# A three-stage kernel with a written instruction order: the list reads of the last expert tiles are gathered into one step ahead of those tiles' weights, and the order is written anew

## The chip, the cores and the metric

The kernel runs on one NeuronCore of a Trainium2 chip. The metric is the device time of one execution in microseconds (us). Before the change three runs gave 534.38, 535.60 and 536.59 us; the median is 535.6. The five engines of the core each work through their own instructions in order: PE (TensorE, matrix multiplication), DVE (VectorE), ACT (ScalarE), POOL (GpSimd, which here also issues the gathers and scatters through an index list) and SP (SyncE, which issues the plain DMAs). They meet only at semaphores.

## The reference

Three stages follow each other. What is computed, cut to its core:

```python
# 1. chunked state-space attention: 4 batches, 8 heads, 768 positions, head size 32, state 16
L = exp(cum[:, None] - cum[None, :]) * causal          # inside a chunk
y = (C @ B.T * L) @ x + (C @ state) * exp(cum)
state = decay * state + (B * decay_from_j).T @ x
x = y.reshape(3072, 256)
# 2. dense layer
h = x @ w_in                                           # 256 -> 2048
x = maximum(0.01 * h, h) @ w_out                       # 2048 -> 256
# 3. one of eight experts for every token
logits = x @ w_gate + modality_bias[modality_id]
e_idx, gate = argmax(logits), softmax(logits)[e_idx]
for e in range(8):
    mask = e_idx == e
    out[mask] = gate * (maximum(x[mask] @ w1[e], 0) @ w2[e])   # 256 -> 1024 -> 256
```

## The kernel before, in words

Stage 1 goes through 24 chunks of 128 positions. Stage 2 goes through six blocks of 512 tokens, each in 16 steps of 128 hidden columns: a step `h` (L655, six matmuls; both operands are split into a high and a low part, so that three products stand for one) and a step `y` (L695, six matmuls). Chunks and blocks are interleaved. After the last `y` of a block its logits are formed, every token gets its expert and its place, and POOL scatters the token numbers into a list in DRAM (`put`, L835: four scatters of 128 numbers, 4 bytes each; the list is `il`). The token rows themselves go to a DRAM buffer `yx`.

Stage 3 takes tiles of 512 tokens of one expert. Two *early* tiles (0 and 1) are taken from the lists of the first four blocks; the *final* tiles (2 to 5 here, and more behind branches that were not taken in this trace) need the lists of all six blocks. For tile `i` the steps are:

- `ix.i` (L962 to L964, SP): reads from a small table which piece of the list the tile has, then issues the DMA of 512 list entries into `gi`. It waits for all scatters of all `put` steps so far (L965 to L969).
- `w1.i`, `w2.i` (L945 to L955, SP): the expert's number from the table, then two DMAs of 512 KB each for `w1` (256x1024) and two for `w2` (1024x256), into raw tiles. Three raw tiles exist, so a load may wait until an earlier raw tile has been converted.
- `ga.i` (L977, POOL): four gathers of 128 token rows each through `gi`, into `xg`.
- `xt.i` (L1006, PE): eight transposes of `xg` into `xps`; `xe`, `xf` (L1012 on ACT, L1016 on DVE): the high and the low part of the tokens, `x2h` and `x2l`.
- `sh1`, `sh2` (L995, ACT) and `sl1`, `sl2` (L999, DVE; the second half of `sl2` on POOL): high and low part of the weights, `w1s` and `w2s`, half by half.
- `m1.i.f` (L1025, PE, six matmuls) for eight hidden groups `f` into `hp`, of which two exist; `re.i.f` (L1039, ACT) and `rl.i.f` (L1043, DVE) make `hh` and `hl` from it and so set `hp` free; `m2.i.f` (L1056, PE, twelve matmuls) adds up the output `o`.
- `oe.i.q` (L1082, ACT) scales the output, `sc.i.q` (L1086, POOL) scatters it to the result.

Nothing is scheduled when the program is built: the string `PLAN` names all steps (1,599 of them) in one line of order, and each engine gets the instructions of a step in that order. `m1.1.3 m2.1.0` in the plan means that PE gets the twelve matmuls of `m2.1.0` behind the six of `m1.1.3`. Where an instruction waits, all that stands behind it on its engine waits too.

Of the kernel before, what the change touches and what calls it, by code (L numbers as in the profile page):

```python
# [41 lines left out]
    trc.5 exp.6.0 subv.i.2.1 cb.5 gl.6 h.8 hb.o.2.1 mul.5.0 mul.5.2 lb.o.2.1 mul.5.1 hb.i.3.0 h.9 mul.5.3 or.o.2.1  # L42
    sa.8 gh.7 y.6 gg.8 lb.i.3.0 cast.o.2.1 gl.7 h.10 sa.9 subv.o.2.1 gh.8 or.i.3.0 hb.i.3.1 trmm.6 p3.5 lb.i.3.1 gl.8
    cast.i.3.0 y.7 or.i.3.1 sa.10 load.9 exp.7.1 gg.9 subg.i.3.0 y.8 cast.i.3.1 gg.10 gh.9 mask.8 trc.6 h.11 hb.o.3.0
    subv.i.3.1 gh.10 gl.9 xa.5 h.12 gl.10 exp.6.1 xb.5 cd.8 y.9 trb.6 bs.6 sa.11 lb.o.3.0 gg.11 cb.6 sa.12 or.o.3.0
    gh.11 h.13 exp.8.0 mul.6.1 mul.6.3 y.10 mul.6.0 cast.o.3.0 mul.6.2 gg.12 sa.13 subg.o.3.0 p3.6 exp.7.0 gl.11
    trmm.7 load.10 xa.6 h.14 st.6 trb.7 trc.7 gh.12 xb.6 hb.o.3.1 bs.7 gl.12 trd.7 y.11 lb.o.3.1 gg.13 trde.7 sa.14
    or.o.3.1 cb.7 exp.8.1 h.15 mul.7.3 gh.13 mul.7.1 mul.7.2 cast.o.3.1 gl.13 y.12 sa.15 mul.7.0 mask.9 gg.14 y.13
    gg.15 gh.14 bs.8 exp.9.1 gl.14 p3.7 cd.9 subv.o.3.1 gh.15 trmm.8 load.11 st.7 xa.7 y.14 trb.8 xb.7 exp.9.0 trc.8
    gl.15 h.16 bs.9 bt h.17 sa.16 gg.16 y.15 sa.17 gh.16 gg.17 h.18 evV.0 evA.0 gh.17 gl.16 trd.8 gl.17 sa.18 h.19  # L50
    trde.8 gg.18 mask.10 lg.0 sa.19 cd.10 exp.10.0 gg.19 y.16 lt.0 exp.10.1 cb.8 y.17 gh.18 mul.8.3 mul.8.1 mul.8.0
    mul.8.2 trmm.9 gh.19 gl.18 p3.8 trb.9 trc.9 gl.19 trd.9 xa.8 load.12 l2.0 y.18 st.8 trde.9 r1.0 trmm.10 xb.8 rx.0
    trd.10 r2.0 trb.10 h.20 trde.10 mask.11 trc.10 r3.0 cb.9 sa.20 bs.10 cd.11 exp.11.1 h.21 gg.20 mul.9.2 mul.9.0
    gh.20 y.19 mul.9.1 sa.21 mul.9.3 gl.20 exp.11.0 p3.9 gg.21 gh.21 rp.0 st.9 load.13 xa.9 yr.0.0 be.0 h.22 yc.0.0
    xb.9 put.0 gl.21 yr.0.1 sa.22 bs.11 h.23 yc.0.1 gg.22 ro.0 h.24 sa.23 gg.23 trmm.11 sa.24 y.20 trc.11 trb.11
    trd.11 gh.22 y.21 trde.11 gl.22 gg.24 cb.10 gh.23 mask.12 y.22 mul.10.3 mul.10.2 exp.12.0 mul.10.1 mul.10.0 h.25
    gl.23 gh.24 exp.12.1 gl.24 p3.10 sa.25 y.23 st.10 load.14 xa.10 gg.25 xb.10 h.26 gh.25 bs.12 gl.25 cb.11 sa.26
    h.27 gg.26 mask.13 mul.11.2 mul.11.0 h.28 mul.11.3 sa.27 mul.11.1 exp.13.0 gg.27 p3.11 cd.13 sa.28 exp.13.1 y.24
    load.15 xa.11 bs.13 y.25 gh.26 xb.11 gl.26 h.29 gh.27 gg.28 gl.27 y.26 sa.29 gg.29 y.27 gh.28 gl.28 h.30 gh.29
    gl.29 h.31 sa.30 gg.30 y.28 sa.31 cd.14 mask.14 gg.31 trmm.12 gh.30 h.32 trc.12 trb.12 gl.30 exp.14.1 cb.12 sa.32  # L60
    h.33 mul.12.1 exp.14.0 mul.12.0 mul.12.3 mul.12.2 y.29 sa.33 gg.32 p3.12 gh.31 gl.31 trmm.13 xa.12 load.16 y.30
    st.12 trb.13 trc.13 mask.15 xb.12 gg.33 y.31 gh.32 bs.14 exp.15.0 gl.32 trd.13 evV.1 h.34 evA.1 cd.15 gh.33 h.35
    sa.34 gl.33 trde.13 gg.34 exp.15.1 y.32 sa.35 cb.13 gg.35 gh.34 h.36 mul.13.3 mul.13.1 mul.13.2 mul.13.0 y.33
    sa.36 gl.34 gg.36 lg.1 gh.35 gl.35 p3.13 lt.1 l2.1 st.13 xa.13 load.17 yr.1.0 r1.1 h.37 yc.1.0 r2.1 rx.1 trmm.14
    sa.37 r3.1 rp.1 trb.14 trc.14 trd.14 y.34 be.1 trde.14 xb.13 put.1 h.38 gg.37 gh.36 bs.15 gl.36 cb.14 sa.38 cd.16
    h.39 gg.38 mul.14.2 mul.14.0 y.35 mul.14.3 sa.39 mask.16 mul.14.1 p3.14 gh.37 exp.16.0 gl.37 yr.1.1 load.18 st.14
    y.36 yc.1.1 gg.39 xa.14 exp.16.1 trmm.15 xb.14 ro.1 y.37 trc.15 trb.15 bs.16 gh.38 trd.15 h.40 gh.39 gl.38 trde.15
    gl.39 cb.15 sa.40 y.38 gg.40 mul.15.3 mul.15.2 mask.17 y.39 mul.15.1 gh.40 mul.15.0 gl.40 exp.17.1 p3.15 cd.17
    exp.17.0 y.40 st.15 load.19 xa.15 bs.17 xb.15 h.41 h.42 sa.41 gg.41 trmm.16 sa.42 h.43 trc.16 gh.41 gg.42 trb.16
    gl.41 gh.42 h.44 sa.43 gl.42 gg.43 y.41 sa.44 mask.18 gg.44 h.45 gh.43 exp.18.1 gl.43 h.46 sa.45 exp.18.0 gg.45  # L70
    y.42 sa.46 y.43 gh.44 gl.44 h.47 gg.46 gh.45 gl.45 y.44 sa.47 gg.47 trd.16 gh.46 y.45 mask.19 trde.16 gl.46 h.48
    gh.47 exp.19.1 gl.47 cb.16 sa.48 y.46 mul.16.3 exp.19.0 mul.16.0 mul.16.1 mul.16.2 y.47 gg.48 gh.48 p3.16 evV.2
    evA.2 gl.48 lg.2 xa.16 load.20 st.16 xb.16 y.48 lt.2 bs.18 l2.2 trmm.17 r1.2 trd.17 trb.17 h.49 trde.17 trc.17
    rx.2 r2.2 cb.17 sa.49 r3.2 cd.19 h.50 gg.49 mul.17.2 gh.49 mul.17.1 h.51 sa.50 mul.17.0 gl.49 gg.50 rp.2 sa.51
    mul.17.3 h.52 gh.50 be.2 gg.51 p3.17 put.2 sa.52 gl.50 y.49 xa.17 load.21 gg.52 xb.17 bs.19 yr.2.0 gh.51 y.50
    yc.2.0 gl.51 trmm.18 gh.52 h.53 trc.18 trb.18 gl.52 cb.18 sa.53 h.54 gg.53 mask.20 mul.18.2 mul.18.3 y.51 mul.18.0
    sa.54 mul.18.1 exp.20.0 gg.54 yr.2.1 cd.20 p3.18 gh.53 yc.2.1 gl.53 y.52 load.22 xa.18 st.18 exp.20.1 xb.18
    trmm.19 gh.54 h.55 trc.19 ro.2 bs.20 trb.19 gl.54 y.53 sa.55 gg.55 h.56 gh.55 gl.55 y.54 sa.56 gg.56 trd.19 y.55
    mask.21 gh.56 trde.19 gl.56 exp.21.1 cb.19 cd.21 h.57 mul.19.3 exp.21.0 mul.19.0 mul.19.2 mul.19.1 h.58 sa.57
    gg.57 p3.19 sa.58 gh.57 gg.58 y.56 load.23 xa.19 gl.57 xb.19 h.59 st.19 gh.58 bs.21 gl.58 h.60 sa.59 gg.59 mask.22  # L80
    y.57 sa.60 gg.60 exp.22.1 h.61 gh.59 y.58 sa.61 gl.59 exp.22.0 gg.61 h.62 gh.60 gl.60 y.59 sa.62 gg.62 h.63 gh.61
    gl.61 y.60 sa.63 gg.63 trmm.20 gh.62 trd.20 trc.20 h.64 trb.20 gl.62 trde.20 cd.22 y.61 sa.64 gg.64 y.62 gh.63
    mask.23 cb.20 gl.63 gh.64 exp.23.1 h.65 mul.20.1 mul.20.2 mul.20.3 exp.23.0 mul.20.0 y.63 gl.64 sa.65 trmm.21
    evV.3 evA.3 p3.20 trb.21 gg.65 h.66 trc.21 xa.20 st.20 gh.65 xb.20 bs.22 trd.21 sa.66 y.64 gl.65 trde.21 gg.66
    cd.23 lg.3 gh.66 gl.66 h.67 lt.3 l2.3 sa.67 y.65 r1.3 gg.67 rx.3 h.68 r2.3 gh.67 r3.3 rp.3 gl.67 sa.68 y.66 be.3
# [1170 lines left out]
```

## Time and profile before

| what | before |
| --- | --- |
| median of 3 runs | 535.6 us (534.38 to 536.59) |
| the profiled execution | 535.73 us, of which 533.9 us lie between its first and last instruction (the span) |
| PE busy | 499.9 us, 94% of the span, 3,266 matmuls |
| weight loads of PE (beside the matmuls) | 396.9 us, 74% |
| DVE, ACT, POOL busy | 331.3, 288.1, 138.3 us |
| granted clock of PE, mean | 0.983 of full speed |
| DMA | 48.4 MB; 84,066 of 120,150 packets under 512 bytes |

The page's row of forty slices shows PE at 9 tenths or more nearly everywhere; the slices that fall out are the first ones, one pair near three quarters of the span, and the last. The row of the granted clock shows a dip in that same pair and at the end.

```profile
PE   8968999999999999999999999999984999999990
PEclk9999999999999999999999999999996999999996
```

An engine that is busy 94% of the time leaves little to gain from faster work on the others; what can be gained is PE's own idle time, and the question for each gap is which engine or transfer ended it.

### The profile page before, as it was taken

The numbers are of one execution on the slowest core, as the hardware profiler recorded it, in microseconds if no ns is written. First come the engines' busy times: TensorE is split into PE (matmuls) and PEld (weight loads), VectorE is DVE, ScalarE is ACT, GpSimd is POOL, SyncE is SP. The second block draws the span as 40 slices with busy tenths as digits, with TensorE's granted clock in tenths as the row PEclk, the third lists the DMA queues.
The fourth block names the chain that finished last, engine by engine and source line by source line (L and its number), as shares of the span: only waits on it lengthen the run. The fifth ranks groups of instructions, "written<-read, shape, count | busy, mean of one in ns | idle before, by whom it ended". The sixth has DMA issues, their size and how long they took to land.

```text
span 533.9 us, 8921 instructions
## 1 busy us (share of the span) xinstructions
PE 499.9 (94%) x3266; PEld 396.9 (74%) x3266; DVE 331.3 (62%) x719; ACT 288.1 (54%) x626; POOL 138.3 (26%) x137
## 2 busy tenths in 40 slices
PE   8968999999999999999999999999984999999990
...
PEclk9999999999999999999999999999996999999996
...
GB/s 200 150 212 205 271 61 66 59 111 58 100 71 60 23 137 2 68 51 150 1 1 49 204 187 1 43 1 1 51 160 247 99 136 166 58 41 39 1 60 25
DMA packets 120150, 48.40 MB, mean 91 GB/s; under 512 B 84066, under 2 KB 113891, under 8 KB 120099
## 3 DMA queue, kind: packets, MB, share of 16 engines
...
q0 software_dynamic: 3072, 6.41, 3.8%
...
HBM read 41.14 MB, written 6.60 MB: 89 GB/s over the span
## 4 chain that ended last, share of the span: by engine, by line
PE 62%; issue 13%; DMA 8%; POOL 5%; DVE 5%; ACT 4%; SPq 1%; POOLq 0%; ACTq 0%; DVEq 0%
PE h L655 24%; PE y L695 23%; POOL out_dram L1086 3%; PE hp L1025 3%; PE cb L512 2%; PE o L1056 2%; PE psy L552 2%; DMA xg<-yx,gi 2%; DMA il<-ids,pi 2%; DMA gi<-il 1%; PE psy L547 1%; DVE gl L677 1%; PE yr L852 1%; DMA e<-cumd 1%; DMA il<-sent 1%
## 5 line engine op out<-in xcount | busy, mean ns | idle before, releaser
L662 ACT ACTIVATE sa<-h 128x512 f32<-128x512 f32 x96 | 56.8, 595 | 74.8 <-PE h L655 73.9
L667 DVE TENSOR_TENSOR gg<-sa,h 128x512 f32<-128x512 f32 x96 | 65.2, 684 | 42.2 <-ACT sa L662 41.8
L677 DVE TENSOR_TENSOR gl<-gg,gh 128x512 fp32r<-128x512 f32 x96 | 75.2, 787 | 14.6 <-ACT gh L672 13.0
L655 PE MATMUL h<-xh,wih 128*128 128x512 f32 x192 | 79.4, 414 | 1.8 <-DVE gg L667 1.7
L695 PE MATMUL y<-gh,woh 128*128 128x512 f32 x192 | 78.7, 410 | 0.0
L655 PE MATMUL h<-xl,wih 128*128 128x512 f32 x192 | 75.2, 392 | 0.9 <-DVE xl L576 0.9
L695 PE MATMUL y<-gl,woh 128*128 128x512 f32 x192 | 75.3, 392 | 0.4 <-DVE gl L677 0.3
L695 PE MATMUL y<-gh,wol 128*128 128x512 f32 x192 | 75.1, 391 | 0.0
L655 PE MATMUL h<-xh,wil 128*128 128x512 f32 x192 | 75.1, 391 | 0.0
L1043 DVE SCALAR_TENSOR_TENSOR hl<-hp,hh 128x512 fp32r<-128x512 f32 x48 | 33.0, 689 | 60.8 <-ACT hh L1039 60.7
L1056 PE MATMUL o<-w2s,hh 128*128 128x256 f32 x384 | 70.0, 282 | 0.0
L672 ACT CAST gh<-gg 128x512 fp32r<-128x512 f32 x96 | 59.0, 617 | 19.2 <-DVE gg L667 10.5
L1025 PE MATMUL hp<-x2h,w1s 128*128 128x512 f32 x192 | 66.1, 398 | 0.0
L1039 ACT ACTIVATE hh<-hp 128x512 fp32r<-128x512 f32 x48 | 28.7, 598 | 63.4 <-PE hp L1025 58.4
L1056 PEld LDWEIGHTS o<-w2s,hh 128*128 128x128 f32 x384 | 61.2, 190 | 2.2
L835 POOL DMA_INDIRECT il<-ids,pi x24 | 24.4, 1017 | 124.3 <-DVE pi L825 60.7
L1056 PE MATMUL o<-w2s,hl 128*128 128x256 f32 x192 | 54.1, 282 | 0.0
L417 ACT ACTIVATE e<-e,ncum 128x128 f32<-128x128 f32 x160 | 50.6, 392 | 2.6 <-POOL e L399 2.6
L655 PEld LDWEIGHTS h<-xh,wih 128*128 128x128 f32 x192 | 36.0, 188 | 15.5 <-DVE gg L667 4.1
L399 POOL TENSOR_SCALAR_AFFINE_SELECT e<-e 128x1024 f32<-128x1024 f32 x20 | 25.0, 1256 | 79.0 <-DMA e<-cumd 45.4
L695 PEld LDWEIGHTS y<-gh,woh 128*128 128x128 f32 x192 | 36.1, 188 | 10.8 <-issue 3.1
L1025 PEld LDWEIGHTS hp<-x2h,w1s 128*128 128x128 f32 x192 | 36.8, 192 | 7.4 <-issue 0.2
...
## 6 DMA issues: line engine op xcount, KB each, us to landing
r<-in_moe_w_dram SPq DMA_DIRECT2D x24, 512.0 KB, 6.1
e<-cumd SPq DMA_DIRECT2D x20, 512.0 KB, 5.1
...
yx<-ysb SPq DMA_DIRECT2D x6, 528.0 KB, 11.2
...
```

The lines of the kernel that those rows point to most:

```text
L399: g.affine_select(out=e, in_=e, pattern=[[0, H], [1, P]], compare_op=ALU.is_ge, fill=NEG, base=0, channel_multiplier=-1)
L417: s.activation(out=e[:, h, :], in_=i, func=AF.Exp, bias=ncum[:, cc, b * H + h:b * H + h + 1])
L655: t_.matmul(h, lhsT=w[:, k, fs], rhs=xx[:, k, :], start=(i == 0), stop=(i == 5))
L662: s.activation(out=d["sa"], in_=d["h"], func=AF.Copy, scale=0.01)
L667: v.tensor_tensor(out=d["gg"], in0=d["sa"], in1=d["h"], op=ALU.max)
L672: s.copy(out=d["gh"], in_=d["gg"])
L677: v.tensor_tensor(out=gl, in0=d["gg"], in1=d["gh"].bitcast(F32), op=ALU.subtract)
L695: t_.matmul(y_t[j][k], lhsT=w[:, f, ds], rhs=gg, start=(f == 0 and i == 0), stop=(f == NF - 1 and i == 2))
L1025: t_.matmul(d["hp", f], lhsT=d[1][:, k, part, fs], rhs=xx[:, k, :], start=(n == 0), stop=(n == 5))
L1039: s.activation(out=e_h(i, f, "hh"), in_=ex[i]["hp", f], func=AF.Relu)
L1043: v.scalar_tensor_tensor(out=e_h(i, f, "hl"), in0=d["hp", f], scalar=0.0, in1=d["hh", f].bitcast(F32), op0=ALU.max, op1=ALU.subtract)
L1056: t_.matmul(d["o", q], lhsT=d[h, f][:, q * P:(q + 1) * P], rhs=d[2][:, f, part, :], start=(start and n == 0), stop=(f == NF2 - 1 and n == ...
```

## The change

Two things are changed. A new step `ixs` issues the list reads of all four final tiles, one behind the other, and stands in the plan in front of `w1.2`; the four steps `ix.2` to `ix.5` are gone. The weight loads behind it come in the order of the tiles: `w1.2 w2.2 w1.3 w2.3 w1.4 ...`, where before `w1.3` stood ahead of `w2.2`. And the whole plan behind its first 248 steps is another order of the same steps, found by a new search. No other instruction is added or removed.

```diff
-    tf2 m1.0.4 tf3 m1.0.5 re.0.4 tf4 m2.0.3 re.0.5 rl.0.4 w1.2 rl.0.5 m2.0.4 ix.2 w1.3 m1.0.6 ix.3 m1.0.7 re.0.6 ix.4
-    rl.0.6 ix.5 m2.0.5 re.0.7 ga.2 rl.0.7 m1.1.0 m1.1.1 re.1.0 rl.1.0 m2.0.6 re.1.1 w2.2 sh1.2.0 rl.1.1 m2.0.7 sh1.2.1
-    sl1.2.0 m2.1.0 oe.0.2 sl1.2.1 oe.0.0 oe.0.1 sc.0.0 m1.1.2 oe.0.3 w2.3 ga.3 xt.2 re.1.2 rl.1.2 m1.1.3 xe.2.1 xe.2.0
...
+    m2.0.5 re.0.7 ixs rl.0.7 m1.1.0 m1.1.1 re.1.0 w1.2 rl.1.0 m2.0.6 re.1.1 w2.2 rl.1.1 m2.0.7 w1.3 m1.1.2 oe.0.0
+    oe.0.1 sc.0.0 oe.0.3 m1.1.3 re.1.2 sc.0.1 oe.0.2 rl.1.2 m2.1.0 re.1.3 ga.2 rl.1.3 m2.1.1 sh1.2.0 m1.1.4 sh1.2.1
...
-        "w1": e_w1, "w2": e_w2, "ix": e_ix, ...
+        "w1": e_w1, "ixs": lambda: [e_ix(i) for i in range(EARLY, EARLY + NSTAT)], "w2": e_w2, "ix": e_ix, ...
```

On SP, behind the last two writes of token rows to `yx`, before:

```order
L864 DMA yx<-ysb 128x4x264 x2
L945 TENSOR_LOAD tabf
L948 ISA
L948 DMA r_4734<-in_moe_w_dram 128x1024
L948 ISA
L948 DMA r_4734<-in_moe_w_dram 128x1024
L962 TENSOR_LOAD tabf
L964 REGISTER_ALU
L964 DMA gi<-il 128x4x1
L945 TENSOR_LOAD tabf
L948 ISA
L948 DMA r_4759<-in_moe_w_dram 128x1024
```

The same place now (four list reads stand between the first and the second weight tile's place):

```order
L864 DMA yx<-ysb 128x4x264 x2
L962 TENSOR_LOAD tabf
L964 REGISTER_ALU
L964 DMA gi<-il 128x4x1
L962 TENSOR_LOAD tabf
L964 REGISTER_ALU
L964 DMA gi<-il 128x4x1
...
L945 TENSOR_LOAD tabf
L948 ISA
L948 DMA r_4818<-in_moe_w_dram 128x1024
```

The read of `w1.2` (the first `r` in each piece) stood ahead of the first list read and now stands behind the fourth.

On PE, around the transposes of tile 2 (`xps`), before; `hp` is the result of an `m1` step, `o` that of an `m2` step, `w1s_4452` and `w2s_4478` are the weights of tile 1:

```order
L1056 MATMUL o_4877<-w2s_4478,hl_4840 128x256
L1025 MATMUL hp_4900<-x2h_4499,w1s_4452 128x512
L1025 MATMUL hp_4900<-x2l_4500,w1s_4452 128x512
L1025 MATMUL hp_4900<-x2h_4499,w1s_4452 128x512 x2
...
L1006 MATMUL xps_4925<-ident_100,xg_4809 128x128 x4
L1006 MATMUL xps_4926<-ident_100,xg_4809 128x128 x4
L1025 MATMUL hp_4941<-x2h_4499,w1s_4452 128x512
L1025 MATMUL hp_4941<-x2l_4500,w1s_4452 128x512
```

and now:

```order
L1025 MATMUL hp_5012<-x2h_4499,w1s_4452 128x512
...
L1056 MATMUL o_4892<-w2s_4478,hh_4953 128x256 x2
L1056 MATMUL o_4892<-w2s_4478,hl_4955 128x256
L1006 MATMUL xps_5040<-ident_100,xg_4907 128x128 x4
L1006 MATMUL xps_5041<-ident_100,xg_4907 128x128 x4
L1056 MATMUL o_4892<-w2s_4478,hh_4985 128x256 x2
L1056 MATMUL o_4892<-w2s_4478,hl_4989 128x256
```

Before, only `m1.1.0` to `m1.1.2` and `m2.1.0` of tile 1 stood ahead of tile 2's transposes; now all eight `m1.1` steps and `m2.1.0` to `m2.1.4` do.

On ACT, the converting casts of `w1.2` and `w2.2` (L995) among the activations of tile 1 (`hh`), now:

```order
L1039 ACTIVATE hh_4905<-hp_4876 128x512
L995 CAST w1s_4934<-r1_4818 128x1024 x2
L1039 ACTIVATE hh_4953<-hp_4936 128x512
L1039 ACTIVATE hh_4985<-hp_4946 128x512
L995 CAST w2s_4987<-r2_4837 128x4x256 x2
L1039 ACTIVATE hh_5019<-hp_5005 128x512
```

The casts of `w1.2` stand ahead of the activations of `m1.1.4` and behind, and those of `w2.2` ahead of that of `m1.1.6`, where ACT would wait for them if the weights were late.

## Rows read from the trace of the kernel before

**Rows 1.** Windows: stretch, its us, busy us of PE, PEld, DVE, ACT, POOL; PEclk, DMA share, GB/s
```profile
62.00:377.00 315.00, 312.52 (x2007) 240.29 (x2006) 226.46 (x513) 187.80 (x432) 58.51 (x49) 1.00 0.40 68
398.00:412.00 14.00, 4.98 (x17) 3.33 (x16) 2.93 (x5) 3.43 (x8) 9.92 (x10) 0.66 0.91 267
412.00:521.00 109.00, 109.00 (x711) 99.55 (x710) 41.14 (x55) 45.67 (x76) 40.21 (x34) 1.00 0.23 77
```
**Rows 2.** Waits of PE: line, what it waited for, us in total, times, longest
```profile
PE xps L1006 <- DMA xg<-yx,gi: 9.0, 4, 5.1
```
**Rows 3.** Timeline of PE from 398 to 415: start, us, instruction, idle before
```profile
398.54 0.39 PE L1025 MATMUL hp<-x2h,w1s 128*128 128x512 f32 x1
...
409.34 1.33 PE L1006 MATMUL xps<-ident,xg 128*128 128x128 f32 x5 [0.71 <-DMA xg<-yx,gi]
410.32 0.78 PE L1025 MATMUL hp<-x2h,w1s 128*128 128x512 f32 x1
...
414.33 0.40 PE L1056 MATMUL o<-w2s,hh 128*128 128x256 f32 x2
```
**Rows 4.** Chain of waits: start, us, what it was spent on
```profile
383.15 9.07 DMA il<-ids,pi
...
403.53 5.77 DMA xg<-yx,gi
```
**Rows 5.** Timeline of SP's DMA issues from 383 to 403
```profile
383.97 0.90 SPq L948 DMA_DIRECT2D r<-in_moe_w_dram  x2
392.36 0.38 SPq L964 DMA_DIRECT2D gi<-il  x1
...
394.61 2.12 SPq L964 DMA_DIRECT2D gi<-il  x3
396.99 5.08 SPq L955 DMA_DIRECT2D r<-in_moe_w_dram  x4
```
**Rows 6.** Timeline of POOL: the first gather of tile 2
```profile
399.34 1.25 POOL L977 DMA_INDIRECT xg<-yx,gi  x1 [15.21 <-DMA gi<-il]
```
**Rows 7.** DMA issues, whole span: count, KB each, median us to landing
```profile
r<-in_moe_w_dram SPq DMA_DIRECT2D x24, 512.0 KB, 6.1
...
il<-ids,pi POOLq DMA_INDIRECT x24, 13.5
xg<-yx,gi POOLq DMA_INDIRECT x24, 5.8
```
**Rows 8.** DMA issues of 383.9 to 384.6 (the two halves of w1.2)
```profile
r<-in_moe_w_dram SPq DMA_DIRECT2D x2, 512.0 KB, 12.4
```
**Rows 9.** DMA issues of 392.3 to 392.5 (the list read of tile 2)
```profile
gi<-il SPq DMA_DIRECT2D x1, 2.0 KB, 6.2
```
**Rows 10.** Chain of waits from 412 on: PE steps that nothing held up
```profile
415.93 1.39 PE hp L1025 x6
417.31 1.43 PE o L1056 x12
...
422.96 0.87 PE xps L1006 x8
```
**Rows 11.** Windows under and behind the list scatters, columns as in Rows 1
```profile
384.00:392.00 8.00, 8.00 (x52) 7.15 (x51) 2.09 (x4) 1.34 (x4) 0.13 (x1) 1.00 1.00 36
396.00:400.00 4.00, 2.93 (x19) 2.32 (x18) 2.45 (x2) 3.70 (x7) 0.66 (x1) 1.00 1.14 331
```
**Rows 12.** Timeline of ACT: the cast of one half of a weight tile
```profile
423.50 1.04 ACT L995 CAST w1s<-r 128x1024 fp32r<-128x1024 f32 x1
```
**Rows 13.** Timeline of DVE: an activation's low part, then one half's low part
```profile
423.63 0.69 DVE L1043 SCALAR_TENSOR_TENSOR hl<-hp,hh 128x512 fp32r<-128x512 f32 x1 [2.14 <-ACT hh L1039]
424.57 1.22 DVE L999 TENSOR_TENSOR w1s<-r,w1s 128x1024 fp32r<-128x1024 f32 x1 [0.24 <-ACT w1s L995]
```
**Rows 14.** Timeline of POOL: first gather of tile 0
```profile
303.76 1.06 POOL L977 DMA_INDIRECT xg<-yx,gi  x1 [19.01 <-DVE xl L576]
```
**Rows 15.** Timeline of PE: first matmul of the first h step of block 5
```profile
316.49 0.39 PE L655 MATMUL h<-xh,wih 128*128 128x512 f32 x1
```

More of the change, by code (lines that the diff above doesn't have):

```diff
@@ L41 @@
     trde.5 exp.5.0 h.7 cd.7 st.4 sa.6 y.4 bs.5 sa.7 gl.5 cast.o.2.0 gg.6 xa.4 y.5 subg.o.2.0 gg.7 gh.6 xb.4 cast.i.2.1
[L42 to L85, printed above, removed]
@@ new lines @@
+    or.o.2.1 sa.8 h.9 lb.i.3.0 gg.8 cast.o.2.1 or.i.3.0 h.10 gh.8 sa.9 subv.o.2.1 exp.6.1 p3.5 gl.7 hb.i.3.1 gg.9
+    trmm.6 load.9 y.7 lb.i.3.1 gl.8 trb.6 cast.i.3.0 or.i.3.1 h.11 sa.10 gh.9 gg.10 subg.i.3.0 cast.i.3.1 y.8 trc.6
+    xa.5 subv.i.3.1 sa.11 mask.8 xb.5 hb.o.3.0 h.12 gh.10 gl.9 lb.o.3.0 gg.11 y.9 exp.7.0 bs.6 gl.10 cb.6 or.o.3.0
+    exp.7.1 h.13 hb.o.3.1 mul.6.0 mul.6.2 cast.o.3.0 mul.6.1 y.10 mul.6.3 lb.o.3.1 subg.o.3.0 gh.11 p3.6 sa.12 bs.7
+    gl.11 sa.13 trmm.7 gg.12 xa.6 load.10 trd.7 trb.7 y.11 trde.7 trc.7 gh.12 xb.6 st.6 exp.8.1 gl.12 h.14 gg.13
@@ new lines @@
+    exp.8.0 or.o.3.1 cb.7 sa.14 y.12 mul.7.1 gh.13 mul.7.2 mul.7.0 cast.o.3.1 h.15 mul.7.3 mask.9 gg.14 subv.o.3.1
+    gh.14 trmm.8 gl.13 p3.7 sa.15 exp.9.0 gl.14 y.13 load.11 cd.8 gg.15 xa.7 trb.8 trc.8 exp.9.1 trd.8 xb.7 y.14 bs.8
+    cd.9 bt trde.8 gh.15 h.16 gl.15 h.17 sa.16 bs.9 st.7 gg.16 cb.8 sa.17 gh.16 y.15 gg.17 mul.8.3 mul.8.2 h.18
+    mul.8.1 evA.0 evV.0 gh.17 mul.8.0 mask.10 h.19 sa.18 gl.16 exp.10.1 lg.0 gg.18 p3.8 sa.19 lt.0 gl.17 exp.10.0
+    cd.10 l2.0 load.12 st.8 trmm.9 trd.9 xa.8 h.20 r1.0 trde.9 trb.9 r2.0 rx.0 y.16 sa.20 xb.8 trc.9 gg.19 rp.0 gh.18
@@ new lines @@
+    r3.0 yr.0.0 be.0 y.17 yc.0.0 mask.11 gl.18 put.0 yr.0.1 exp.11.1 h.21 gg.20 gh.19 cd.11 bs.10 y.18 yc.0.1 gl.19
+    sa.21 ro.0 exp.11.0 gg.21 trmm.10 trd.10 y.19 trc.10 trde.10 gh.20 trb.10 h.22 gl.20 gh.21 gl.21 h.23 sa.22 gg.22
+    cb.9 sa.23 y.20 gg.23 mul.9.3 mul.9.2 y.21 mul.9.1 gh.22 mul.9.0 gl.22 p3.9 mask.12 gh.23 trmm.11 st.9 xa.9
+    load.13 trd.11 trb.11 h.24 xb.9 trde.11 exp.12.1 trc.11 bs.11 gl.23 cb.10 sa.24 y.22 exp.12.0 mul.10.3 mul.10.1
+    mul.10.2 mul.10.0 h.25 gg.24 gh.24 p3.10 sa.25 gl.24 gg.25 y.23 xa.10 load.14 st.10 xb.10 h.26 bs.12 gh.25 gl.25
@@ new lines @@
+    cb.11 sa.26 h.27 gg.26 mul.11.2 mul.11.1 y.24 mul.11.3 sa.27 mul.11.0 gg.27 p3.11 gh.26 gl.26 y.25 xa.11 load.15
+    xb.11 h.28 gh.27 gl.27 y.26 sa.28 cd.13 gg.28 mask.13 y.27 gh.28 exp.13.1 gl.28 h.29 exp.13.0 h.30 sa.29 bs.13
+    gg.29 y.28 sa.30 gh.29 gg.30 h.31 gl.29 gh.30 cd.14 gl.30 y.29 sa.31 mask.14 gg.31 trmm.12 exp.14.1 h.32 trc.12
+    gh.31 y.30 trb.12 gl.31 sa.32 exp.14.0 gg.32 cb.12 y.31 gh.32 mul.12.3 mul.12.2 mul.12.0 mask.15 mul.12.1 h.33
+    evA.1 evV.1 gl.32 exp.15.0 lg.1 sa.33 p3.12 lt.1 exp.15.1 gg.33 l2.1 st.12 load.16 trmm.13 r1.1 xa.12 h.34 trb.13
@@ new lines @@
+    gh.33 r2.1 rx.1 xb.12 y.32 sa.34 trc.13 r3.1 gg.34 rp.1 gl.33 h.35 gh.34 be.1 trd.13 sa.35 h.36 gl.34 put.1
+    trde.13 gg.35 cb.13 bs.14 sa.36 cd.15 y.33 gg.36 mul.13.1 mul.13.0 h.37 mul.13.2 gh.35 mul.13.3 gl.35 p3.13 sa.37
+    gg.37 yr.1.1 xa.13 load.17 st.13 y.34 yc.1.1 xb.13 bs.15 yr.1.0 gh.36 h.38 yc.1.0 gl.36 ro.1 y.35 sa.38 gg.38
+    trmm.14 gh.37 trd.14 trc.14 h.39 trde.14 gl.37 trb.14 cd.16 mask.16 cb.14 sa.39 y.36 gg.39 exp.16.1 mul.14.2
+    mul.14.3 h.40 mul.14.0 gh.38 mul.14.1 exp.16.0 gl.38 p3.14 sa.40 y.37 st.14 xa.14 load.18 xb.14 gg.40 y.38 gh.39
@@ new lines @@
+    bs.16 gl.39 trmm.15 gh.40 trd.15 trc.15 h.41 trb.15 gl.40 trde.15 cb.15 sa.41 h.42 gg.41 mask.17 mul.15.3 mul.15.2
+    y.39 mul.15.0 sa.42 mul.15.1 exp.17.0 gg.42 p3.15 cd.17 gh.41 exp.17.1 y.40 gl.41 load.19 st.15 xa.15 bs.17 h.43
+    gh.42 xb.15 gl.42 h.44 sa.43 gg.43 y.41 sa.44 gg.44 y.42 gh.43 gl.43 h.45 gh.44 gl.44 y.43 mask.18 sa.45 gg.45
+    exp.18.1 h.46 gh.45 h.47 sa.46 gl.45 exp.18.0 gg.46 y.44 sa.47 y.45 gg.47 gh.46 gl.46 trmm.16 gh.47 h.48 trc.16
+    trb.16 gl.47 trd.16 sa.48 y.46 mask.19 trde.16 gg.48 cb.16 gh.48 exp.19.1 h.49 mul.16.3 mul.16.1 mul.16.0 exp.19.0
@@ new lines @@
+    gl.48 y.47 mul.16.2 sa.49 p3.16 evV.2 evA.2 gg.49 lg.2 xa.16 load.20 st.16 gh.49 xb.16 h.50 lt.2 gl.49 bs.18 l2.2
+    sa.50 trmm.17 r1.2 trd.17 trb.17 h.51 trde.17 r2.2 rx.2 trc.17 rp.2 sa.51 r3.2 trmm.18 be.2 y.48 trb.18 trc.18
+    put.2 gg.51 cb.17 gg.50 y.49 mul.17.2 gh.50 mul.17.3 mul.17.0 h.52 gh.51 mul.17.1 gl.50 gl.51 p3.17 sa.52 cd.19
+    gg.52 yr.2.1 xa.17 load.21 bs.19 y.50 yc.2.1 xb.17 h.53 gh.52 gl.52 cb.18 sa.53 y.51 gg.53 mul.18.2 mul.18.1 h.54
+    mul.18.3 gh.53 mul.18.0 mask.20 yr.2.0 sa.54 gl.53 p3.18 yc.2.0 gg.54 exp.20.0 ro.2 trmm.19 load.22 st.18 y.52
```

76 lines of the change are left out of this document (43 added, 33 removed).

## The prediction, made before the changed kernel was run

> **What bounds the kernel now.** I read the page's busy shares first: PE works in 94% of the span, so only PE's own gaps are worth time. The windows tell where they lie [rows 1]: from 62 to 377 us PE is busy 312.5 of 315 us, from 412 to 521 it is never idle, and between them, from 398 to 412, it works 5.0 of 14 us at a granted clock of 0.66. The list of PE's waits then names the gap: the transposes of tile 2 waited for the gather of its tokens, 9.0 us in four pieces [rows 2]. The timeline shows what stands around them [rows 3]: the last matmul ahead ends at 398.54 + 0.39 = 398.93, the last five transposes start at 409.34, and the first matmul behind starts at 410.32. That one, `m1.1.3`, belongs to tile 1 and needs nothing of tile 2: PE waited with work that was ready behind the waiting instruction.
>
> Backwards from there the chain is [rows 4 to 6]: the last gather took 5.77 us from 403.53; the first gather was issued at 399.34, when the list entries of tile 2 had come; these were asked for at 392.36 and took 6.2 us [rows 9]; and they were asked for when the scattered list had landed, 9.07 us after the last scatter's issue at 383.15.
>
> **The change part by part.** *PE's order.* Before, PE does `m1.1.0` to `m1.1.2` and `m2.1.0` ahead of tile 2's transposes. Now `m1.1.3` to `m1.1.7` and `m2.1.1` to `m2.1.4` stand ahead too. An `m1` step takes 1.39 us and an `m2` step 1.43 when nothing holds PE [rows 10], so this is 5 x 1.39 + 4 x 1.43 = 12.7 us of work, and PE comes to the transposes at 398.93 + 12.7 = 411.6. Even if the tokens came no earlier than before (409.3, the end of the last gather), they would be there 2.3 us ahead.
>
> What that gives back: from 398.93 to 410.32 are 11.39 us, of which the eight transposes need 0.87 [rows 10], so 10.5 us. And the two `m1` steps behind the gap ran from 410.32 to 414.33, 4.01 us where 2 x 1.39 = 2.78 would do; the granted clock was 0.66 over the stretch and full in the next [rows 1], PE having been idle before it fell. Without the gap that is another 1.2 us. Together 11.7 us.
>
> *The list reads ahead of the weights.* SP still cannot ask for tile 2's entries before the scatters have landed at 392.2; the read is issued no earlier. What goes is the traffic ahead of it on its queue. The trace has no list read on a free queue: it lies between the 6.2 us measured and next to nothing, so the entries come between 392.4 and 398.5. I take 6.2, the nearest row, and nothing of the sum hangs on it: on POOL two output scatters of tile 0 now stand ahead of the gathers, and they wait for tile 0's outputs, whose last matmuls end at about 398.93 - 1.39 - 1.43 = 396.1 on PE (`m1.1.2` and `m2.1.0` came behind them). With half a microsecond for the scaling and two scatters at the gathers' pace, (403.53 - 399.34) / 3 = 1.4 us each, the first gather is issued near 399.4, as before, the fourth near 403.6, and with 5.8 us [rows 7] it ends at 409.4. The cover is PE's 12.7 us; where it is gone, each microsecond of a later gather past 411.6 costs one.
>
> *The weights behind the list reads.* This is the price. `w1.2` was issued at 383.97, now it stands behind four list reads. Three of these took 2.12 us on SP, 0.87 apart [rows 5], so the fourth is issued at 392.4 + 3 x 0.87 = 395.0, and the halves of `w1.2` at about 395.9 and 396.5: 12 us later. The early issue had brought little: its halves took 12.4 us [rows 8], since the DMA engines moved 36 GB/s from 384 to 392, under the scatters, and 331 GB/s after [rows 11]. That is 0.29 of its 1.05 MB, worth 0.9 us at the later rate. The Trainium skill (DMA: Bandwidth & Descriptors, section on queues, rings and completion order) says that a DMA engine goes round between the queues that have work, packet by packet; by this rule the weights would have had half of the engines beside the scatters, all of `w1.2` would have been in before 392, and holding it back would cost its full 1.05 MB, 3.2 us of transfer. The trace disagrees with an even share: 36 GB/s is a ninth of the later rate, not half.
>
> When is `w1.2` needed? ACT casts it ahead of `re.1.4`, and ACT and DVE are in order, so late weights hold up tile 1's activations. Behind what was done at 398.93 come `m1.1.3`, `m2.1.1`, `m1.1.4`, `m1.1.5`, `m2.1.2` and `m2.1.3`, 3 x 1.39 + 3 x 1.43 = 8.5 us, and then, at 407.4, `m1.1.6`. It needs the buffer that `rl.1.4` frees. Behind the second half's landing come its cast (1.04), its low part (1.22) and `rl.1.4` (0.69) [rows 12, 13], 2.95 us, so the half must land by 404.4. With the median 6.1 us of a weight load [rows 7] it lands at 402.6, 1.8 us ahead; with the 12.4 us of [rows 8] at 408.9, and PE waits 4.5 us. I take 6.1, since nothing scatters any more then. `w2.2` and `w1.3` follow 1.1 us apart in issue; at 331 GB/s each needs 3.2 us, so they land near 406 and 409, and their first users on PE come at 415 (tile 2's first `m1`) or later. Cost: zero, upper bound 4.5.
>
> *The rest of the order.* PE has the same instructions; from 62 to 377 us only 2.5 us of idle time can be won [rows 1]. A new order may as well add waits; the trace prices none of them, and I take twice today's, 5 us, as the other end, and zero as the value. Tile 0's transposes move most, to the place of the `y` step ahead of block 5's first `h`. That `h` began at 316.49 [rows 15], so with one step of six matmuls less PE comes to them at 315.1. Tile 0's gathers start at 303.76 [rows 14], the fourth some 4.2 us later, and with 5.8 us [rows 7] end at 313.8, 1.3 us ahead of PE. The last steps of tile 5 keep their chain: final matmul, scaling, scatter. Zero.
>
> Sum: 535.73 (profiled execution) - 10.5 - 1.2 = 524.0. The median of the runs, 535.6, lies 0.1 below the profiled one, so no correction.
>
> **The rivals.** *Part of the gap stays.* The list lands later: over all scatters the median is 13.5 us [rows 7]. If the last one takes that, all moves by 4.4 us: the gathers end near 413.5, and the weights' second half lands at 407. PE waits 2 us at the transposes or 2.5 at `m1.1.6`, one in place of the other, and loses a little clock: 527. For it: [rows 7]; against it: the measured 9.07 had the weights beside it, which are gone.
>
> *The new order loses in the long middle.* The bound above: 524 + 5 = 529. For it: tile 0's margin of 1.3 us; against it: only 2.5 us of waits in 315.
>
> *The gap moves.* The work drawn ahead is missing later, and PE waits at tile 2's first `m1` or tile 3's transposes for what it formerly had time to wait for: 535. For it: the same 12.7 us can fill only one hole; against it: tile 3's gathers follow tile 2's at once and end near 414, and PE gets to its transposes at 411.6 + 0.87 + 2 x 1.43 + 1.39 = 416.7.
>
> *Slower: ACT stands behind the weights.* Each tile of 1 MB takes the 12.4 us of [rows 8] behind the four list reads, instead of 6.1 and overlapped. Then `w1.2`, `w2.2` and `w1.3` come at 408, 421 and 433; ACT casts `w1.3` ahead of tile 2's `x2h`, so the first `m1` of tile 2, due at 415.4, starts at about 437. That is 21 us more: 545. It is slower than before once a tile takes over 9.5 us (`w1.3` in at 424, 11.7 us lost). For it: three waits of ACT for DMA stand ahead of PE's work; against it: 331 GB/s as soon as the scatters are through.
>
> **How the numbers follow.** The forecast 524.0 has 0.63, with its own range of 521.5 to 526; part of the gap 0.18; the middle lost 0.08; the gap moved 0.05; slower 0.04; better than 521.5 (the middle's 2.5 us won whole) 0.02. The range 521 to 529 takes in the forecast, the first two rivals, and leaves out about one in ten. Half a per cent, 2.7 us, is what a measurement of this kernel tells from no change: faster than 533 has 0.91, within 0.05, slower 0.04.
>
> **What would show it.** Right: no PE wait for the gather at tile 2's transposes, which start near 411 (shifted by what the middle changes), granted clock 1.00 from 398 to 412, `w1.2` issued about 3.5 us behind the first list read, PE's busy time about 499, and the idle time between 377 and the end down to that of the last scatters. Wrong: ACT waiting for a weight load with `m1.1.6` waiting for `rl.1.4`; a PE wait at tile 0's or tile 3's transposes; more than 5 us of idle time between 62 and 377.

## The result, and the profile after

The changed kernel takes 521.12 us (median of four runs, 520.77 to 522.35); the kernel before took 534.99 us beside it. The ratio is 0.974, with a 95% interval of 0.971 to 0.977: 2.6% less time. The profiled execution took 520.77 us, its span is 519.1 us, and TensorE's mean granted clock 0.988.

The windows of the kernel after, columns as in [rows 1]:

```profile
62.00:377.00 315.00, 313.82 (x2026) 242.43 (x2026) 225.91 (x526) 189.20 (x433) 59.78 (x50) 1.00 0.36 69
398.00:412.00 14.00, 14.00 (x98) 13.02 (x97) 8.41 (x11) 7.57 (x11) 11.09 (x10) 1.00 0.96 327
412.00:508.00 96.00, 94.31 (x614) 85.66 (x613) 34.75 (x46) 39.52 (x68) 36.25 (x31) 1.00 0.24 79
```

From 398 to 412 us PE is now busy for 14.00 of 14 us at the full clock, where it was 4.98 at 0.66. (Its last matmul ends at 506.4, hence the 94.31 in the last row.) The wait of [rows 2] is not in the list of PE's waits any more, whose longest entry, in the head of the kernel (ahead of 64 us), is now

```profile
PE cb L512 <- ACT btt L471: 1.7, 2, 1.1
```

and PE's timeline, which answers to [rows 3], shows the eight transposes of tile 2 in one piece (408.32) with no idle time ahead of them; those at 413.47 are tile 3's:

```profile
408.20 0.28 PE L1056 MATMUL o<-w2s,hl 128*128 128x256 f32 x1
408.32 1.04 PE L1006 MATMUL xps<-ident,xg 128*128 128x128 f32 x8
409.12 0.48 PE L1056 MATMUL o<-w2s,hh 128*128 128x256 f32 x2
...
412.08 0.40 PE L1025 MATMUL hp<-x2h,w1s 128*128 128x512 f32 x1
...
413.47 1.03 PE L1006 MATMUL xps<-ident,xg 128*128 128x128 f32 x8
```

SP's DMA issues, to be held against [rows 5]; `gi` is a list read, `r` a weight load. All four list reads now stand ahead of the first weights:

```profile
388.35 2.99 SPq L964 DMA_DIRECT2D gi<-il  x4
391.93 0.89 SPq L948 DMA_DIRECT2D r<-in_moe_w_dram  x2
393.01 0.96 SPq L955 DMA_DIRECT2D r<-in_moe_w_dram  x2
394.55 0.89 SPq L948 DMA_DIRECT2D r<-in_moe_w_dram  x2
```

What became of these two kinds, from the lists of DMA issues of 388.3 to 391.1 and of 391.8 to 392.6 us (count, KB each, median us from issue to landing); they answer to [rows 8, 9]:

```profile
gi<-il SPq DMA_DIRECT2D x4, 2.0 KB, 2.2
...
r<-in_moe_w_dram SPq DMA_DIRECT2D x2, 512.0 KB, 4.4
```

A list read lands in 2.2 us instead of 6.2, and the halves of `w1.2` in 4.4 us instead of 12.4 (medians; the second half, issued at 392.48, took 4.9 us and landed at 397.36). POOL's timeline has the scatters of tile 0's output and then the first gather, which stood at 399.34 before [rows 6]:

```profile
393.12 0.98 POOL L1086 DMA_INDIRECT out_dram<-o,gi  x1 [12.03 <-ACT o L1082]
394.41 0.98 POOL L1086 DMA_INDIRECT out_dram<-o,gi  x1 [0.31 <-issue]
395.69 1.05 POOL L977 DMA_INDIRECT xg<-yx,gi  x1 [0.30 <-issue]
```

To see where the time came from, cut the span at a matmul that both orders have in the same place with the same work behind it: the first matmul of the last rank step (`rp`, L804), of which the row is, after,

```profile
373.93 0.19 PE L804 MATMUL rp<-ohb,tris 128*128 128x32 bf16 x1
```

and before it started at 376.96. Between it and PE's last matmul lie 874 matmuls in either kernel. The windows of the late part, and of the middle part that begins at the first `cb` step behind 64 us (64.70 before, 64.41 after), first of the kernel before,

```profile
64.70:376.96 312.26, 310.30 (x1997) 238.98 (x1997) 223.72 (x507) 185.64 (x427) 57.21 (x48) 1.00 0.40 66
376.96:521.05 144.09, 135.07 (x874) 122.24 (x872) 54.69 (x96) 54.98 (x92) 54.05 (x47) 0.96 0.37 99
```

then of the kernel after:

```profile
64.41:373.93 309.52, 309.15 (x1997) 238.93 (x1998) 220.84 (x507) 186.13 (x427) 57.74 (x48) 1.00 0.36 67
373.93:506.37 132.44, 132.38 (x874) 120.66 (x872) 54.74 (x96) 55.11 (x92) 54.43 (x47) 1.00 0.33 108
```

The late part is 144.09 - 132.44 = 11.65 us shorter: of 9.02 us of idle time (144.09 - 135.07) 0.06 are left, and the same 874 matmuls take 132.38 us instead of 135.07, 2.69 us less; the granted clock of the late part is 1.00 now, where it was 0.66 from 398 to 412 us. The middle is 2.74 us shorter: 1.96 us of idle time became 0.37, and PE is busy 1.15 us less with the same 1997 matmuls. The head, all that lies ahead of that `cb` step, gives 0.29. Together 14.7 us, and PE's last matmul ends at 506.37 instead of 521.05.

### The profile page after: what moved, and what is told of

Its sections match the earlier page's. It is cut to its first block, busy times and chain, and to the rows that moved or that the text cites. A ratio compares the mean times of both kernels' runs of the same rounds, so it can differ in the third digit from the quotient of the medians.

```text
span 519.1 us, 8927 instructions
## 1 busy us (share of the span) xinstructions
PE 494.6 (95%) x3263; PEld 393.6 (76%) x3266; DVE 328.2 (63%) x719; ACT 288.4 (56%) x626; POOL 137.9 (27%) x137
## 4 chain that ended last, share of the span: by engine, by line
PE 78%; issue 8%; DVE 4%; POOL 3%; ACT 3%; DMA 1%; POOLq 0%; ACTq 0%; DVEq 0%; SPq 0%
PE y L695 24%; PE h L655 24%; PE hp L1025 9%; PE o L1056 9%; PE cb L512 2%; PE psy L552 2%; POOL out_dram L1086 2%; PE psy L547 1%; PE xps L1006 1%; PE yr L852 1%; DMA e<-cumd 1%; DVE hb L605 1%; DVE hb L606 1%; PE lp L734 1%; DVE gg L667 1%
## 5 line engine op out<-in xcount | busy, mean ns | idle before, releaser
L677 DVE TENSOR_TENSOR gl<-gg,gh 128x512 fp32r<-128x512 f32 x96 | 71.2, 748 | 14.9 <-ACT gh L672 14.0
L655 PEld LDWEIGHTS h<-xh,wih 128*128 128x128 f32 x192 | 36.0, 188 | 12.7 <-DVE gg L667 2.9
L695 PEld LDWEIGHTS y<-gl,woh 128*128 128x128 f32 x192 | 36.1, 188 | 8.4 <-DVE gl L677 2.3
```

Of the source, the lines that this page charges most:

```text
L655: t_.matmul(h, lhsT=w[:, k, fs], rhs=xx[:, k, :], start=(i == 0), stop=(i == 5))
L677: v.tensor_tensor(out=gl, in0=d["gg"], in1=d["gh"].bitcast(F32), op=ALU.subtract)
L695: t_.matmul(y_t[j][k], lhsT=w[:, f, ds], rhs=gg, start=(f == 0 and i == 0), stop=(f == NF - 1 and i == 2))
```

## The experiments

In what follows the *late part* is the time from the last rank step's first matmul to PE's last. It does not depend on how the head went, whose first `h` matmul starts at 36.9 to 40.8 us in the profiled executions. Its time splits into idle and busy time of PE. What PE is busy over 132.4 us is for the most part the slow clock, though not in all: in two executions below (SP's order undone and the late order alone, the first of each) PE was busy 0.8 and 1.1 us longer while the granted clock of the late part was 1.00. Ratios are to the kernel before on the same chip in the same series of runs; its median was 536.4 us beside the first four kernels, 536.2 beside the next four and 534.3 beside the last three, while most expectations count from 535.0, so ratios are what to compare.

**Is it the late order or the middle?** One kernel has the old order up to step `re.0.3` (1290 steps; the last rank step, `rp.5`, follows eight steps later in either order) and the new one from there, another the reverse. Both halves hold the same steps, so they can be joined.

```diff
 # late_only: the plan
-  steps 0 to 1289 as in the changed kernel
+  steps 0 to 1289 as in the kernel before
   steps from 1290 on as in the changed kernel (ixs, w1.2, w2.2, w1.3, ...)
 # early_only: the plan
   steps 0 to 1289 as in the changed kernel
-  steps from 1290 on as in the changed kernel
+  steps from 1290 on as in the kernel before
```

> The new order up to re.0.3, behind it the old order with the old list reads. Theory: only what the middle gives, 1.7 us between the first h step and the last rank step: 533.3 us (532.5 to 534.5), and tile 2's transposes wait 9 us as before. Rival (the 1.3 us that the changed kernel gained ahead of its first h step belong to the order too): 532 us.

> The old order up to and with the last routing steps (re.0.3), the new order with the gathered list reads behind it. Theory (the gap at tile 2's transposes is closed by the order of the last part, 11.7 us): 535.0 - 11.7 = 523.3 us, between 522.5 and 524.3; no PE wait for the gather. Rival (the middle's new order carries a good part of the gain): 526 us or more.

The new middle alone: 534.3 us, ratio 0.996 (0.995 to 0.998), and its list of PE's waits has the gap back:

```profile
PE xps L1006 <- DMA xg<-yx,gi: 8.8, 4, 4.8
```

The new late part alone: 527.9 us, ratio 0.983 (0.979 to 0.987). That is less gain than expected (0.978), and it is the figure of the rival, that the middle carries a good part. Its profiled execution had a late part of 134.87 us, with 1.4 us of waits that the changed kernel doesn't have, and a head 2.7 us longer. So the kernel was run once more:

> The old order up to the last rank matmul, the new one behind it, once more. Its first ratio was 0.983 where the loss of the wait alone gives 0.978, its head ran 2.7 us late, and ScalarE's evictions came 3 to 4.5 us behind TensorE at 409 to 412 us. If the two parts of the change need each other, the late part comes to 134.9 us again and the ratio to 0.983. If both were events of that execution: 132.5 us, ratio 0.977 to 0.979.

524.0 us, ratio 0.980 (0.977 to 0.983). The windows of its middle and of its late part:

```profile
64.81:377.47 312.66, 310.33 (x1998) 239.00 (x1998) 224.98 (x507) 185.84 (x427) 57.08 (x48) 1.00 0.39 67
377.47:509.90 132.43, 132.37 (x874) 120.66 (x872) 54.86 (x96) 55.21 (x92) 54.40 (x47) 1.00 0.33 108
```

The late part is that of the changed kernel to the hundredth, and the middle is that of the kernel before, 0.4 us longer. The two parts add up: by the runs 10.6 us (0.0199 of 534) and 2.0 us (0.0037 of 536), 12.6 together, by the traces 11.65 and 2.7, 14.4 together; the change as a whole gave 13.9, and 15.1 when it was run again. My expectation for the late part alone (0.978) lies inside the second interval and just outside the first. That the first run lost time to an event of its own, and not to a lack of the new middle, rests on the second trace: its late part is whole with the old middle in place.

**Is it the work ahead of the transposes?** In the changed kernel I move tile 2's transposes forward nearly to where the old order had them in relation to tile 1's work (behind `m2.1.0`, with `m1.1.3` alone in addition ahead of them), 11.3 us of PE's work earlier. The list reads, the gathers and the weights stay.

```diff
-  ... re.1.3 ga.2 rl.1.3 m2.1.1 ... m2.1.4 sh1.3.1 re.1.7 xt.2 sh1.3.0 ...
+  ... re.1.3 ga.2 xt.2 rl.1.3 m2.1.1 ... m2.1.4 sh1.3.1 re.1.7 sh1.3.0 ...
```

> The changed kernel with one PE step moved: tile 2's transposes stand 11.3 us of PE work earlier (behind m2.1.0 instead of m2.1.4); SP's order is the changed one. Theory (the work ahead of the transposes is what hides the gather): PE waits there for the gather some 9 us, the clock falls, 531 us (529.5 to 532.5). Rival (the list reads ahead of the weights bring the gather early): wait of at most 4 us, 525 us or less.

533.3 us, ratio 0.993 (0.990 to 0.995), as expected of the theory (531 on 535.0 is 0.9925). PE's waits, and PE's timeline at the transposes:

```profile
PE xps L1006 <- DMA xg<-yx,gi: 7.7, 4, 5.1
```

```profile
403.16 0.45 PE L1006 MATMUL xps<-ident,xg 128*128 128x128 f32 x1 [5.09 <-DMA xg<-yx,gi]
...
407.16 1.33 PE L1006 MATMUL xps<-ident,xg 128*128 128x128 f32 x5 [1.48 <-DMA xg<-yx,gi]
```

Moving one step loses nearly three quarters of the gain by the runs. The rows tell the margin too: all tokens were there at 407.2 us, in an execution whose last rank step came 0.8 us later than the changed kernel's; there the transposes start at 408.32, some 2 us behind the tokens. The late part took 145.06 us, 12.6 more: 8.1 us idle and 4.5 us longer busy, with the granted clock at 0.67 from 398 to 412 us.

**What is SP's order worth?** Once undone in the changed kernel, once done alone in the kernel before.

```diff
 # sp_undone: the changed kernel, PE's order unaltered
-  ... ixs ... w1.2 ... w2.2 ... w1.3
+  ... w1.2 ix.2 w1.3 ix.3 ix.4 ix.5 ... w2.2
 # sp_only: the kernel before, PE's order unaltered
-  ... w1.2 ... ix.2 w1.3 ... ix.3 ... ix.4 ... ix.5 ... w2.2
+  ... ixs w1.2 ... w2.2 ... w1.3
```

> The changed kernel with the list reads and weight loads of tiles 2 and 3 on SP in the old order (w1.2, list 2, w1.3, lists 3 to 5, w2.2); PE's and all other orders as in the changed kernel. Theory (PE's order alone closes the gap; gathers wait for the scatters of tile 0 on POOL anyway): 521.1 us, within 0.8; the list read of tile 2 takes 6 us again and PE still doesn't wait at tile 2's transposes. Rival (the list reads' place makes the gather early enough): 525 us, with a wait of some 4 us at tile 2's transposes.

> The kernel before with only SyncE's part of the change: all four list reads ahead of the weights, weights in the order of tiles; TensorE's order as before. My theory (the work put ahead of tile 2's transposes fills the wait, the reads only bring the gathers some 4 us forward): lists land 2.2 us after issue in place of 6.2, the gathers start about 4 us earlier, but TensorE, which reaches the transposes at 398.9 us, still waits some 5 to 6 us there, then finds weights that are later; about 531 on 535.0, ratio 0.993. Rival A, the list reads carry the gain: about 524, ratio 0.98 or less. Rival B, TensorE's order carries everything: 535, ratio 1.00.

Undone: 523.5 us, ratio 0.974 (0.972 to 0.976), the same as that of the change. But the late part of its profiled execution took 135.83 us, with 2.6 us of waits. ACT's timeline there:

```profile
397.29 1.99 ACT L995 CAST w1s<-r 128x1024 fp32r<-128x1024 f32 x2
405.53 0.60 ACT L1039 ACTIVATE hh<-hp 128x512 fp32r<-128x512 f32 x1 [6.25 <-remote]
408.37 0.60 ACT L1039 ACTIVATE hh<-hp 128x512 fp32r<-128x512 f32 x1 [2.24 <-remote]
```

The matmuls whose results these two evict had started at 399.5 and 400.9, so ACT came 4 us or more late, and not behind a weight. (`remote` means that the profile names no instruction as the releaser, so it does not tell whether ACT or its release was late.) The repetition:

> The changed kernel with SyncE's order as it was before (tile 2's first weights ahead of its list, the other lists behind tile 3's first weights), once more. What is open: its first profile showed the last rank matmul to TensorE's last matmul at 135.8 us against 132.4 of the changed kernel, with ScalarE's evictions of tile 1's fourth and fifth block at 405.5 and 408.4 us, 4 us behind the matmuls that they wait for; the timed runs showed no loss (ratio 0.974). If SyncE's order costs that, the late part comes to 135.8 us again and the ratio is above that of the changed kernel by 0.005 (0.979). If it was an event of that one execution: 132.4 us and ratio 0.973.

520.9 us, ratio 0.975 (0.972 to 0.978), and the late part 132.44 us, with ACT on time:

```profile
397.62 1.99 ACT L995 CAST w1s<-r 128x1024 fp32r<-128x1024 f32 x2
401.39 0.60 ACT L1039 ACTIVATE hh<-hp 128x512 fp32r<-128x512 f32 x1 [1.78 <-PE hp L1025]
402.75 0.60 ACT L1039 ACTIVATE hh<-hp 128x512 fp32r<-128x512 f32 x1 [0.76 <-PE hp L1025]
```

The list read of tile 2, behind the weights again, took 5.0 us there, and PE did not wait for it. So the late evictions do not belong to SP's order; the first profile of the late order alone shows the like (evictions 3 to 4.5 us late at 409 to 412 us), two of thirteen executions in all, and what they are stays open. SP's order as such shows no cost and no gain once PE's order is the new one: the late part is equal, and the ratios (0.974 and 0.975, against 0.974 and 0.972 of the changed kernel) can't be told apart. Done alone it does help: 532.4 us, ratio 0.992 (0.990 to 0.995), as expected. PE's waits and POOL's first gather:

```profile
PE xps L1006 <- DMA xg<-yx,gi: 5.3, 3, 3.5
```

```profile
396.24 1.05 POOL L977 DMA_INDIRECT xg<-yx,gi  x1 [11.46 <-DMA gi<-il]
```

The gathers start 3.1 us sooner than in [rows 6] and PE waits 5.3 us instead of 9.0. Of the 3.7 us of waiting that went, the late part keeps 2.8 (141.31), since PE was busy 0.9 us longer; by the runs the gain is 4.1 us (0.0077 of 536). The gain is there only where PE waits; with the work ahead of the transposes it is not.

**How late may the weights be?** The changed kernel with 8 or 16 more list reads behind the four, into a tile that nothing uses; every weight load of the final tiles is asked for that much later.

```diff
-  "ixs": lambda: [e_ix(i) for i in range(EARLY, EARLY + NSTAT)],
+  "ixs": lambda: [e_ix(i) for i in range(EARLY, EARLY + NSTAT)] + [e_ix2(8)],   # or 16
```

> The changed kernel with eight further list reads (into a tile that nothing uses) behind its four, so that every weight of the final tiles is asked for 7.0 us later (8 x 0.87 us between issues). My theory (the weights' lateness is covered by 4 us of slack and no more): the second half of tile 2's first weights lands at about 404.4, is ready 3 us after TensorE wants it, tile 3's first weights cost about one more: 4 us slower than the changed kernel, 525 on 535.0, ratio 0.981. Rival, weights are never late enough to matter there: 521, ratio 0.974.

> As the run with eight further reads, with sixteen: weights 13.9 us later. My theory: 4 us of it are covered, some 10 us show as waits of TensorE for weights between 400 and 420 us, and the granted clock falls for a moment: 531 to 533 on 535.0, ratio 0.993 to 0.996, nearly all of the gain lost. Rival, lateness is hidden: 521, ratio 0.974.

527.6 us, ratio 0.983 (0.978 to 0.987), and 534.5 us, ratio 0.997 (0.995 to 0.999). ACT's timeline with eight reads shows it standing at the casts of `w1.2`, with two evictions behind them in its queue (lines are 7 further down in this kernel):

```profile
396.50 0.60 ACT L1046 ACTIVATE hh<-hp 128x512 fp32r<-128x512 f32 x1 [0.41 <-PE hp L1032]
404.31 1.05 ACT L1002 CAST w1s<-r 128x1024 fp32r<-128x1024 f32 x1 [7.21 <-DMA r<-in_moe_w_dram]
405.57 1.05 ACT L1002 CAST w1s<-r 128x1024 fp32r<-128x1024 f32 x1 [0.21 <-DMA r<-in_moe_w_dram]
406.52 1.08 ACT L1046 ACTIVATE hh<-hp 128x512 fp32r<-128x512 f32 x2
```

and PE waits at the first matmul of `m1.1.6`, with eight reads

```profile
408.53 0.80 PE L1032 MATMUL hp<-x2h,w1s 128*128 128x512 f32 x1 [3.57 <-DVE hl L1050]
```

and with sixteen, in the list of waits:

```profile
PE hp L1032 <- DVE hl L1050: 10.6, 1, 10.6
```

With eight, PE starts 2.99 us behind the landing of the second half of `w1.2` (405.54); with sixteen, 2.98 behind 412.04. That is the 2.95 us of cast, low part and `rl.1.4` in the prediction. In the changed kernel `m1.1.6` starts at 404.14 and the half landed at 397.36, so the slack is 404.14 - 2.99 - 397.36 = 3.8 us, and past it each microsecond costs one. The windows of the late part, with 8 and with 16:

```profile
374.44:513.46 139.02, 135.39 (x874) 122.82 (x872) 54.54 (x96) 55.23 (x92) 54.77 (x47) 0.98 0.33 103
```

```profile
374.06:520.15 146.09, 135.44 (x874) 122.84 (x872) 54.51 (x96) 55.14 (x92) 54.12 (x47) 0.95 0.34 98
```

I had expected 4 and 10 us for the waits, which they are (3.6 and 10.6), though one of the 4 was to come from tile 3's weights, and all 3.6 came at `m1.1.6`. For the smaller one I had expected no slow clock. It came with both (granted clock 0.50 from 408 to 412 us in either), and PE was busy 3.0 us longer each time (135.4 - 132.4).

**Does the order of the weights matter?** In the changed kernel `w1.3` goes ahead of `w2.2` again, the list reads stay first.

```diff
-  ... ixs ... w1.2 ... w2.2 rl.1.1 m2.0.7 w1.3
+  ... ixs ... w1.2 ... w1.3 rl.1.1 m2.0.7 w2.2
```

> The changed kernel with the last two weights of this place exchanged again (tile 3's first ahead of tile 2's second), the list reads still first. My theory (what counts is that nothing on ScalarE waits for a weight ahead of an eviction): tile 2's second weights land about 404.6 in place of 401.3 us, ScalarE's cast of them, which stands ahead of tile 1's sixth eviction (405.7 us), ends at 406.7: about 1 us, 522 on 535.0, ratio 0.976. Rival, the order of the weights is worth as much as the list reads or more: 525 or above, ratio 0.981.

521.3 us, ratio 0.976 (0.973 to 0.979), and a late part of 132.44 us. The second half of `w2.2` lands at 405.1 (expected 404.6), and ACT's eviction behind it ends at 406.7, but no matmul of PE waits for it: PE needs that eviction later than I took, and the 1 us that I expected is not there. No effect on the late part; the ratio can't be told apart from the changed kernel's.

**The changed kernel once more**, beside three of these (SP's order alone, 8 and 16 reads):

> The changed kernel once more, unaltered, beside the other three of this call. Both theories: ratio to the kernel before 0.974, as measured (521.1 on 535.0). From the head (before the first experts' matmul at 37 to 41 us) executions differ by up to 3 us, so its profiled span may lie between 519 and 523; from the last rank matmul at 373.9 us to TensorE's last matmul I expect 132.4 us again.

521.1 us, ratio 0.972 (0.968 to 0.976), late part 132.44 us. All profiled executions, in us (idle and busy are PE's, in the late part):

```
kernel                    middle   late part   idle    busy
before                    312.3    144.09       9.0   135.07
early order only          309.7    144.91       9.3   135.61
SP's order only           312.6    141.31       5.4   135.95
transposes early          310.0    145.06       8.2   136.89
8 reads more              309.8    139.02       3.6   135.39
16 reads more             309.7    146.09      10.7   135.44
SP's order undone, 1st    310.0    135.83       2.6   133.20
SP's order undone, 2nd    309.8    132.44       0.1   132.38
weights exchanged         309.7    132.44       0.1   132.38
late order only, 1st      312.4    134.87       1.4   133.45
late order only, 2nd      312.7    132.43       0.1   132.37
changed, 1st              309.5    132.44       0.1   132.38
changed, 2nd              309.8    132.44       0.1   132.38
```

(The middle begins at a `cb` step that waits for DVE; in the second execution with SP's order undone it did not wait and is taken from its start at 65.42 us, with the same 1997 matmuls behind it.)

## Why the prediction was right, point by point

**The number, and what of it was luck.** The mechanism of the forecast held: the late part lost the 11.7 us that were forecast, for the reason that was given. The time came out lower than the forecast's own range of 521.5 to 526, in the outcome "better than 521.5" that had a chance of 0.02, and it lies only 0.12 us above the lower end of the wide range, 521. That it lies inside at all is luck; what took it to the edge is above all the term for the middle, below.

**The gap and its size.** Forecast: 10.5 us of waiting and 1.2 of slow clock, 11.7 together, between [rows 3]'s 398.93 and 414.33. Measured over the late part: 9.02 us of idle time and 2.69 of slow clock, 11.65. The two divide the sum in different ways, since in the gap of [rows 3] the transposes themselves ran at the slow clock. That the work put ahead is what closes the gap is shown by the moved transposes (7.7 us of waiting back, 12.6 us in the late part), and that SP's part is not needed by its undoing. That the moved transposes alone, in an otherwise old order of ACT, DVE and POOL, would do as well, no run shows.

**When PE comes to the transposes.** Forecast 411.6, 2.3 us behind the tokens; measured 408.32, that is 411.35 when the 3.03 us by which the last rank step came sooner are put back. The margin came out at about 2 us.

**The list reads.** I took 6.2 us for a read, the upper end, and said that nothing hangs on it. They took 2.2, and with SP's order undone tile 2's took 5.0; the late part is 132.44 us with either. The first gather came at 395.69, or 398.7 with the 3.03 put back, where I had 399.4: as forecast, the two output scatters of tile 0 set it. With SP's order undone the first gather stands in the same place, 21.76 us behind the last rank step in either (375.21 to 396.97; 373.93 to 395.69).

**The weights.** Forecast: the second half of `w1.2` lands 1.8 us ahead of need, at no cost; measured 3.8 us ahead, since the list scatters landed 1.0 us sooner (14.2 us behind the last rank step, before 15.3) and the load took 4.9 us where I took 6.1. The place of the risk was right, and the chain of 2.95 us was 2.98 in the two delayed kernels. The sentence that the early issue of `w1.2` under the scatters had brought little (0.9 us) holds by the landings, though not by the time of the run with that issue restored, which the slack would keep equal either way. In its second execution the second half landed 3.8 us behind the scatters, in the kernel before 5.1; in the changed kernel it is 9.2, of which 3.6 us lie between the first list read and `w1.2`. So the early issue was worth an estimated 5.6 - 5.1 = 0.5 to 5.6 - 3.8 = 1.8 us, and not the 3.2 of an even share of the engines. The rival "ACT stands behind the weights" is real as a mechanism, as the two delayed kernels show, and needs weights 3.8 us later than they come.

**The middle order: the term that was mis-sized.** I took zero between -2.5 and +5. The middle gave 2.7 us in the traces (312.3 to 312.7 in all with the old order, 309.5 to 310.0 in all with the new) and 2.0 in the runs of that part alone. 1.6 us of it are waits; the other 1.15 us are shorter busy time of the same matmuls, which I had not counted as something to be won. Nearly all of that, 1.0 us, is in one kind of matmul of the `h` steps (`h<-xh,wih`, 72.6 us before and 71.6 after, 176 in either); what makes it shorter stays open. From the forecast's 524.0 to the profiled 520.77 are 3.2 us: the middle makes 2.74 of them and the head 0.29. Tile 0's transposes, whose margin I had at 1.3 us, waited for nothing:

```profile
312.46 1.03 PE L1006 MATMUL xps<-ident,xg 128*128 128x128 f32 x8
```

**The rivals.** "Part of the gap stays" and "the gap moves" fall with the windows above: no idle time from 377 to the end but 0.06 us. "The middle loses" falls with its sign. The late list of "part of the gap stays" did not come either: the list scatters landed 8.0 us after the last issue (380.12 to 388.15), where it needed 13.5. "Slower" needed 12.4 us for each weight tile, one behind the other; here the second halves of `w1.2`, `w2.2` and `w1.3` landed at 397.36, 401.30 and 404.61, less than 4 us apart.
